# Moving the twiddle factors of a two-stage Fourier transform from the first-stage to the second-stage matrices

The kernel runs on one core of a Trainium2 chip. The metric is the time of one execution on the device, in microseconds (us).

## The reference

Eight sequences of 3008 tokens with 256 channels are filtered in frequency space, and the result goes through two matrix products.

```python
X = np.fft.rfft(x, axis=1)                      # x: (8, 3008, 256)
Y = X * (filt_r + 1j * filt_i)[None, :, :]
y = np.fft.irfft(Y, n=3008, axis=1)
h = y.reshape(24064, 256) @ w_in                # 256 -> 2048
out = np.maximum(0.01 * h, h) @ w_out           # 2048 -> 256
```

## The kernel before

3008 is 94 x 32. The first stage is a sum over 94 points on TensorE, the second a sum over 32 points. Between them each value is multiplied by a twiddle factor, a complex number of modulus 1 that depends on its place in both stages. Before, it stands in the first-stage matrices: one 94 x 128 matrix for each of the 32 columns of x, 786 KB in all. The second stage has one 128 x 128 matrix.

Batch 0 is transformed alone, ahead of everything else. Batches 1 to 7 are transformed in small groups between the matmuls of the two products (called MoE here).

```python
for i in range(FP):                                          # FP = 4 pieces on SyncE's queue
    nc.sync.dma_start(f1_sb[:, ts(i, step), :], f1_d.ap()[i])
nc.sync.dma_start(small_sb[:], small_d.ap())
first_parts = ((0, 10), (10, 10), (20, 8), (28, 4))          # columns of x: parts 0 to 3
for n0, nn in first_parts:
    x_load(0, n0, nn)                                        # GpSimd's queue, f32 to f16
for hf in range(2):                                          # filter halves 0 and 1
    filt_load(fa_sb, filt_r, hf * DH, DH)
    filt_load(fb_sb, filt_i, hf * DH, DH)
...
keep_warm(28)                                                # matmuls on zeros
for n0, nn in first_parts:
    # first stage of this part, copies out of PSUM by VectorE and ScalarE
    keep_warm(5 if n0 < N2 else 14)
t1_part(0, 0, True)(), t1_part(0, 1, True)()                 # transposes on VectorE
# load of the inverse matrices i1, second stage with filter products,
# inverse stages, then the MoE loop
```

The warm-up matmuls are there to keep TensorE's clock up while it waits for x.

Of the kernel before, what the change touches and what calls it, by code (L numbers as in the profile page):

```python
# [10 lines left out]
P = 128  # L11
FP16 = mybir.dt.float16
# [6 lines left out]
N1, N2 = 94, 32  # L19
NC = 24  # L20
Q = 32
R1 = 96
FP = 4


def _build_np_constants(N):
    n1, n2 = np.arange(N1), np.arange(N2)
    h = N2 // 2

    k2 = np.concatenate([np.arange(h), np.arange(N2 - 1, h - 1, -1)])  # L30

    sg = np.where(k2 < h, 1.0, -1.0)[None, :]
    th = 2 * np.pi * np.outer(n2, k2) / N2
    co, si = np.cos(th), np.sin(th)

    fwd1 = np.zeros((R1, N2, P))
    inv1 = np.zeros((P, N2, N1))
    fwd2, inv2 = np.zeros((P, P)), np.zeros((P, P))

    for s, (qr, qi) in enumerate(((0, 2), (1, 3))):  # L40
        k1 = NC * s + np.arange(NC)

        w = np.where((k1 == 0) | (k1 == N1 // 2), 1.0, 2.0)[:, None] / N1
        for j in n2:
            ang = 2 * np.pi * (np.outer(n1, k1) / N1 + j * k1[None, :] / N)
            fwd1[:N1, j, qr * Q : qr * Q + NC] = np.cos(ang)
            fwd1[:N1, j, qi * Q : qi * Q + NC] = -np.sin(ang)
            inv1[qr * Q : qr * Q + NC, j, :] = w * np.cos(ang).T
            inv1[qi * Q : qi * Q + NC, j, :] = -w * np.sin(ang).T

        cr, ci = (slice(64 * i + s, 64 * i + 64, 2) for i in range(2))
        r, i = (slice(Q * q, Q * q + Q) for q in (qr, qi))
        fwd2[r, cr], fwd2[i, cr] = co, si
        fwd2[r, ci], fwd2[i, ci] = -si * sg, co * sg
        inv2[cr, r], inv2[ci, r] = co.T, -(si * sg).T
        inv2[cr, i], inv2[ci, i] = si.T, (co * sg).T
    inv2 /= N2

    inv2x = np.concatenate([inv2[64:], -inv2[:64]], axis=0)
    small = np.stack([fwd2, inv2, inv2x], axis=1)  # L60
    fwd1 = fwd1.reshape(R1, FP, N2 // FP, P).transpose(1, 0, 2, 3)
    return (np.ascontiguousarray(fwd1).astype(np.float16), inv1.astype(np.float16), small.astype(np.float16))


@with_exitstack
def kernel(
# [9 lines left out]
    nc = tc.nc  # L76
    B, N, D = x.shape
# [7 lines left out]
    assert NCHUNK * CH == TOK  # L85
    SL = 8

    f1_np, i1_np, small_np = _build_np_constants(N)
    f1_d = nc.inline_tensor(f1_np, name="fwd1_const")
    i1_d = nc.inline_tensor(i1_np, name="inv1_const")  # L90
    small_d = nc.inline_tensor(small_np, name="small_const")

    cpool = ctx.enter_context(tc.tile_pool(name="const", bufs=1))
    f1_sb = cpool.tile([R1, N2, P], FP16, name="f1_sb")
    i1_sb = cpool.tile([P, N2, N1], FP16, name="i1_sb")
    small_sb = cpool.tile([P, 3, P], FP16, name="small_sb")
    fa_sb = cpool.tile([P, NC, D], FP16, name="fa_sb")
# [3 lines left out]
    x_sb = cpool.tile([P, N2, D], FP16, name="x_sb")  # L101
# [15 lines left out]
    def bank(kind, n, w):  # L117
        of = wide if kind == "ph" else single
        t = of[turn[kind] % len(of)]
        turn[kind] += 1  # L120
        return t[:, : n * w].rearrange("p (n w) -> p n w", n=n)

    ctx.enter_context(tc.manual_schedule())

    fwd2, inv2, inv2x = (small_sb[:, i, :] for i in range(3))

    DH = D // 2

# [8 lines left out]
    def filt_load(dst, src, d0, dn):  # L137

        for q, first, sgn in ((0, 0, 1), (Q, N1, -1)):
            nc.gpsimd.dma_start(  # L140
                dst[q : q + Q, :, ds(d0, dn)],
                bass.AP(tensor=src.tensor, offset=src.offset + first * D + d0,
                        ap=[[N1 * D, N2 // 2], [sgn * NC * D, 2], [sgn * D, NC], [1, dn]]))


    step = N2 // FP
    for i in range(FP):
        nc.sync.dma_start(f1_sb[:, ts(i, step), :], f1_d.ap()[i])
    nc.sync.dma_start(small_sb[:], small_d.ap())
    first_parts = ((0, 10), (10, 10), (20, 8), (28, 4))  # L150
    for n0, nn in first_parts:
# [1 line left out]
    for hf in range(2):  # L153
        filt_load(fa_sb, filt_r, hf * DH, DH)
        filt_load(fb_sb, filt_i, hf * DH, DH)
    nc.gpsimd.dma_start(w_in_sb[:], moe_w_in.rearrange("(dt p) c -> p dt c", p=P))
    idle = cpool.tile([P, CH], FP16, name="idle")
    nc.vector.memset(idle[:], 0.0)
# [8 lines left out]
    def s1_group(b, g, copy=nc.scalar.copy):  # L167
        def go():
            ps = bank("pf", 2, D)
            for j in range(2):  # L170
                n2 = 2 * g + j
                nc.tensor.matmul(ps[:, j, :], f1_sb[:N1, n2, :], x_sb[:N1, n2, :],  # L172
                                 start=True, stop=True)
            spread(big[(4 * b) % 3], 2 * g, ps, copy)
        return go


    def paired(t):
        return t[:].rearrange("p (e n t) -> p n e t", n=Q, t=2)

    def spread(dst, n0, ps, copy, e0=0):
        nn, de = ps.shape[1], ps.shape[2] // 2
        copy(paired(dst)[:, ds(n0, nn), ds(e0, de)], ps.rearrange("p n (e t) -> p n e t", t=2))  # L183
# [24 lines left out]
    def s2_group(b, g):  # L208
        def go():
            ps = bank("pf", 2, D)  # L210
            src = big[(4 * b + 1) % 3][:].rearrange("p (n d) -> p n d", n=Q)
            nc.tensor.matmul(ps, fwd2, src[:, ds(2 * g, 2), :], start=True, stop=True)  # L212
            fa, fb = fa_sb[:, ds(2 * g, 2), :], fb_sb[:, ds(2 * g, 2), :]
            p1 = scrp.tile([P, 2, D], FP32, tag="p1", name=f"p1_b{b}_g{g}")
            p2 = scrp.tile([P, 2, D], FP32, tag="p2", name=f"p2_b{b}_g{g}")
            nc.vector.tensor_tensor(p1[:], ps, fa, AL.mult)  # L216
            nc.vector.tensor_tensor(p2[0:64], ps[64:P], fb[64:P], AL.mult)  # L217
            nc.vector.tensor_tensor(p2[64:P], ps[0:64], fb[0:64], AL.mult)  # L218
            y1 = ypp.tile([P, 2, D], FP16, tag="y", name=f"y_b{b}_g{g}")
            nc.gpsimd.tensor_tensor(y1[:], p1[:], p2[:], AL.add)  # L220
            ys[(b, g)] = y1
        return go
# [25 lines left out]

    def first_s1(n0, n, kind, copy):
        ps = bank(kind, n, D)  # L250
        for j in range(n):
            nc.tensor.matmul(ps[:, j, :], f1_sb[:N1, n0 + j, :], x_sb[:N1, n0 + j, :],  # L252
                             start=True, stop=True)
        spread(big[0], n0, ps, copy)

# [5 lines left out]
    def first_s2(hf, c, n, kind, on_pool=False):  # L261
        ps = bank(kind, n, DH)
        src = paired(big[1])
        for j in range(0, n, 4):
            nc.tensor.matmul(ps[:, ds(j, 4), :].rearrange("p n (e t) -> p n e t", t=2), fwd2,  # L265
                             src[:, ds(c + j, 4), ts(hf, DH // 2)], start=True, stop=True)
        fs = [f[:, ds(c, n), ts(hf, DH)] for f in (fa_sb, fb_sb)]
        y = [prods[hf][:, i, ds(c, n), :] for i in range(2)]
        if on_pool:
            xs = [scrp.tile([P, 4, DH], FP32, tag=f"p{j // 4 + 1}", name=f"fx_h{hf}_c{c + j}")  # L270
                  for j in range(0, n, 4)]
            for j, xf in enumerate(xs):
                act(xf[:], ps[:, ts(j, 4), :])
            for i in range(2):
                for j, xf in enumerate(xs):
                    nc.gpsimd.tensor_tensor(y[i][:, ts(j, 4), :], xf[:], fs[i][:, ts(j, 4), :], AL.mult)
        else:
            for i in range(2):
                nc.vector.tensor_tensor(y[i], ps, fs[i], AL.mult)  # L279
# [28 lines left out]
    def upper(hf, t, copy):  # L308
        copy(t[64:P, :, ts(hf, DH)], t[0:64, :, ts(hf, DH)])


    def keep_warm(n):
        for _ in range(n):
            nc.tensor.matmul(po_ps.rearrange("p a d -> p (a d)"), idle[:, 0:P], idle[:],  # L314
                             start=True, stop=True)

    keep_warm(28)
    g = 0
    for n0, nn in first_parts:
        while nn:  # L320
            n = 2 if nn % 4 or n0 >= N2 - 4 else 4
            first_s1(n0, n, two[n // 4], (dve, act)[g % 2])
            n0, nn, g = n0 + n, nn - n, g + 1
        keep_warm(5 if n0 < N2 else 14)
    t1_part(0, 0, True)(), t1_part(0, 1, True)()

    nc.vector.memset(i1_sb[:, 0, 0:2], 0.0)
    nc.sync.dma_start(i1_sb[:], i1_d.ap())
    upper(0, fa_sb, act), upper(0, fb_sb, dve)
    first_s2(0, 8, 8, "ph", True)  # L330
    t1_part(0, 2, True)()
    first_s2(0, 0, 8, "ph")
    for n0 in (0, N2 // 2):
        x_load(1, n0, N2 // 2)
    t1_part(0, 3, True)()
    upper(1, fa_sb, act)
    first_s2(0, 16, 4, "pf"), first_s2(0, 20, 4, "pf")
    upper(1, fb_sb, dve)
    keep_warm(4)
# [89 lines left out]
    for slot in range(SL * (NCHUNK + 1)):  # L429
        ci, g = divmod(slot, SL)  # L430
# [36 lines left out]
```

## Time and profile before

| | before |
|---|---|
| time, median of the first 3 runs | 783.67 us (783.07 to 783.7) |
| span of the profiled execution | 780.9 us |
| TensorE busy | 771.9 us, 99% of the span |
| first MoE matmul starts | 41.50 us |
| from there to the end | 739.4 us |

### The profile page before, as it was taken

To read this page: it belongs to the slowest core of one execution; us is meant where nothing else is said; L and a number is where in the kernel's file an instruction comes from. 1 tells how busy PE (TensorE), PEld (TensorE's weight loads), DVE (VectorE), ACT (ScalarE), POOL (GpSimd) and SP (SyncE) were. 2 spreads that over 40 slices of the span, in tenths; PEclk is the share of its full clock that TensorE was granted. 3 is DMA by queue.
4 is the path that set the end of the run, shared out by engine and by line. 5 is a ranking of instruction groups with operands and counts; after the bars stand their busy time and mean duration, and the time that the engine had idled before them with its cause. 6 is when DMAs were issued, how large, how long until landed. Compare 5 with 4: busy or idle time off the path is not lost.

```text
span 780.9 us, 13401 instructions
## 1 busy us (share of the span) xinstructions
PE 771.9 (99%) x5710; PEld 523.9 (67%) x5710; DVE 369.5 (47%) x468; ACT 553.7 (71%) x784; POOL 146.4 (19%) x120
## 2 busy tenths in 40 slices
PE   9899999999999999999999999999999999999998
PEld 4366677666776677666777667766677666766666
DVE  4979751865238641576307744087432765200000
ACT  4777768676786767777587776967668776666664
POOL 4764300340004300042002410025000330000000
PEclk9999999999999999999999999999999999999999
DMA  9942003310141101510105010140101001110111
GB/s 189 217 79 74 28 28 68 82 38 32 41 95 42 42 28 42 108 41 29 41 28 122 28 42 28 41 107 28 42 28 42 28 31 38 41 38 31 41 41 55
DMA packets 36364, 43.38 MB, mean 56 GB/s; under 512 B 8146, under 2 KB 34386, under 8 KB 35538
## 3 DMA queue, kind: packets, MB, share of 16 engines
q0 software_dynamic: 9968, 16.22, 12.2%
q1 hardware_dynamic: 26336, 26.30, 9.6%
q8 instruction: 44, 0.72, 0.4%
q14 instruction: 16, 0.13, 0.1%
HBM read 34.10 MB, written 24.64 MB: 75 GB/s over the span
## 4 chain that ended last, share of the span: by engine, by line
PE 94%; ACT 1%; DVE 1%; issue 0%
PE ph L375 41%; PE po_ps L389 41%; PE pf L172 3%; PE pf L239 2%; PE pf L227 2%; PE pf L212 2%; PE pf L389 1%; ACT big L183 0%; DVE prod L279 0%; PE pf L286 0%; DVE big L294 0%; PE ph L303 0%; ACT yt L306 0%; ACT gt_c L380 0%; PE ph L265 0%
## 5 line engine op out<-in xcount | busy, mean ns | idle before, releaser
L380 ACT ACTIVATE gt_c<-ph 128x1024 f16<-128x1024 f32 x376 | 385.2, 1025 | 195.2 <-PE ph L375 193.8
L375 PE MATMUL ph<-yt,w_in_sb 128*128 128x512 f16 (+3 forms) x1600 | 386.4, 366 | 0.3
L389 PE MATMUL po_ps<-w_out_sb,gt_c 128*128 128x256 f16 x2944 | 381.5, 272 | 0.5 <-ACT ost_c_t L396 0.5
L389 PEld LDWEIGHTS <-gt_c 128*128 128x128 f16 x3008 | 290.8, 98 | 89.2 <-issue 1.8
L375 PEld LDWEIGHTS <-w_in_sb 128*128 128x128 f16 x1600 | 154.5, 98 | 95.7 <-issue 0.4
L220 POOL TENSOR_TENSOR y_b_g<-p_b_g,p_b_g 128x512 f16<-128x512 f32 x84 | 106.9, 1272 | 225.0 <-DVE p_b_g L218 225.0
L195 DVE STREAM_TRANSPOSE big<-big 128x1024 f32<-128x1024 f32 x32 | 55.9, 1846 | 126.1 <-ACT big L183 126.1
L183 ACT CAST big<-pf 128x512 f16<-128x512 f32 x186 | 106.5, 603 | 1.1 <-PE pf L252 1.1
L242 DVE CAST yt<-pf 128x376 f16<-128x376 f32 x112 | 56.4, 545 | 86.1 <-PE pf L239 86.1
L216 DVE TENSOR_TENSOR p_b_g<-pf,fa_sb 128x512 f32<-128x512 f32 x84 | 58.1, 692 | 37.7 <-PE pf L212 35.1
L396 ACT COPY ost_c_t<-po_ps 128x256 f32<-128x256 f32 x184 | 69.3, 376 | 6.5 <-PE po_ps L389 5.3
L203 DVE STREAM_TRANSPOSE big<-big 128x1024 f32<-128x1024 f32 x28 | 51.0, 1933 | 34.4 <-ACT big L183 34.4
L217 DVE TENSOR_TENSOR p_b_g<-pf,fb_sb 64x512 f32<-64x512 f32 x84 | 58.2, 692 | 1.1
L218 DVE TENSOR_TENSOR p_b_g<-pf,fb_sb 64x512 f32<-64x512 f32 x84 | 57.4, 683 | 1.1
L132 POOL DMA_DIRECT2D x_sb<-in_x_dram x13 | 7.1, 548 | 253.9 <-PE pf L172 253.1
L239 PEld LDWEIGHTS <-big 128*128 128x128 f16 x448 | 25.6, 98 | 13.2
L172 PE MATMUL pf<-x_sb,f_sb 94*128 94x256 f16 x224 | 33.9, 272 | 0.2 <-DVE yt L242 0.2
L212 PE MATMUL pf<-big,small_sb 128*128 128x512 f16 x84 | 31.8, 379 | 0.0
L227 PE MATMUL pf<-y_b_g,small_sb 128*128 128x512 f16 x84 | 31.8, 379 | 0.0
L172 PEld LDWEIGHTS <-f_sb 94*128 94x128 f16 x224 | 21.5, 97 | 12.4 <-issue 0.4
L239 PE MATMUL pf<-i_sb,big 128*128 128x94 f16 x448 | 28.7, 206 | 0.0
L314 PE MATMUL po_ps<-idle 128*128 128x512 f16 x66 | 17.5, 414 | 1.2 <-DVE one L161 1.2
(49 smaller groups left out, 157.9 us busy)
## 6 DMA issues: line engine op xcount, KB each, us to landing
out_dram<-ost_c_t SPq DMA_DIRECT2D x92, 256.0 KB, 2.1
x_sb<-in_x_dram POOLq DMA_DIRECT2D x5, 1536.0 KB, 10.9
x_sb<-in_x_dram POOLq DMA_DIRECT2D x2, 768.0 KB, 9.7
x_sb<-in_x_dram POOLq DMA_DIRECT2D x3, 480.0 KB, 8.8
w_in_sb<-in_moe_w_in_dram POOLq DMA_DIRECT2D x1, 1024.0 KB, 14.7
w_out_sb<-in_moe_w_out_dram POOLq DMA_DIRECT2D x1, 1024.0 KB, 9.7
x_sb<-in_x_dram POOLq DMA_DIRECT2D x1, 1024.0 KB, 8.2
f_sb<-fwd_const SPq DMA_DIRECT2D x4, 192.0 KB, 5.5
```

What stands on the lines that cost most here:

```text
L172: nc.tensor.matmul(ps[:, j, :], f1_sb[:N1, n2, :], x_sb[:N1, n2, :], start=True, stop=True)
L183: copy(paired(dst)[:, ds(n0, nn), ds(e0, de)], ps.rearrange("p n (e t) -> p n e t", t=2))
L216: nc.vector.tensor_tensor(p1[:], ps, fa, AL.mult)
L217: nc.vector.tensor_tensor(p2[0:64], ps[64:P], fb[64:P], AL.mult)
L218: nc.vector.tensor_tensor(p2[64:P], ps[0:64], fb[0:64], AL.mult)
L220: nc.gpsimd.tensor_tensor(y1[:], p1[:], p2[:], AL.add)
L239: nc.tensor.matmul(ps[:, j, :], src[:, dt, n2, :], i1_sb[:, n2, :], start=True, stop=True)
L242: copy(yv[:, :, ds(4 * h, 4)], ps.rearrange("p c a -> p a c"))
L375: nc.tensor.matmul(ph[:, j, ds(o, ln)], w_in_sb[:, dt, ts(ct, P)], yt[:, dt, ds(lo, ln)], start=(dt == 0), stop=(dt == NDT - 1),)
L380: nc.scalar.activation(gts[ci][:, ds(2 * g, 2), :], ph, AF.Lrelu)
L389: nc.tensor.matmul(po, gts[ci][:, ct, ts(tj, P)], w_out_sb[:, ct, :], start=(ct == 0), stop=(ct == NCT - 1))
L396: nc.scalar.copy(ost[:, tj % 2, :], po)
```

## The change

The intent: with the twiddle in the second stage, the first stage needs a single matrix, which fits into the 96 KB of small matrices. So x can load with nearly nothing beside it, and the new second-stage matrices (24 of 128 x 128, again 786 KB) come later, behind filter half 0. The warm-ups ahead of the first part go from 28 to 14, as x is expected earlier, and the inverse matrices are released later. The core of the diff (the numpy that builds the matrices, the renamings, and the same two edits in batch 0's own two stages are cut):

```diff
-    step = N2 // FP
-    for i in range(FP):
-        nc.sync.dma_start(f1_sb[:, ts(i, step), :], f1_d.ap()[i])
     nc.sync.dma_start(small_sb[:], small_d.ap())
...
         filt_load(fb_sb, filt_i, hf * DH, DH)
+        for i in (1, 0, 2) if hf == 0 else ():
+            nc.gpsimd.dma_start(f2_sb[:, ts(i, NC // FP), :], f2_d.ap()[i])
...   first stage, batches 1 to 7
-            for j in range(2):
-                n2 = 2 * g + j
-                nc.tensor.matmul(ps[:, j, :], f1_sb[:N1, n2, :], x_sb[:N1, n2, :], start=True, stop=True)
+            nc.tensor.matmul(ps, fwd1[:N1], x_sb[:N1, ds(2 * g, 2), :], start=True, stop=True)
...   second stage, batches 1 to 7
-            nc.tensor.matmul(ps, fwd2, src[:, ds(2 * g, 2), :], start=True, stop=True)
+            for j in range(2):
+                nc.tensor.matmul(ps[:, j, :], f2_sb[:, 2 * g + j, :], src[:, 2 * g + j, :],
+                                 start=True, stop=True)
...   head
-    keep_warm(28)
+    keep_warm(14)
...
     t1_part(0, 0, True)(), t1_part(0, 1, True)()
-    nc.vector.memset(i1_sb[:, 0, 0:2], 0.0)
-    nc.sync.dma_start(i1_sb[:], i1_d.ap())
     upper(0, fa_sb, act), upper(0, fb_sb, dve)
     first_s2(0, 8, 8, "ph", True)
     t1_part(0, 2, True)()
     first_s2(0, 0, 8, "ph")
+    nc.vector.memset(i1_sb[:, 0, 0:2], 0.0)
+    nc.sync.dma_start(i1_sb[:], i1_d.ap())
```

More of the change, by code (lines that the diff above doesn't have):

```diff
@@ L22 @@
 R1 = 96
-FP = 4
+FP = 3
 def _build_np_constants(N):
@@ L34, in _build_np_constants @@
     co, si = np.cos(th), np.sin(th)
-    fwd1 = np.zeros((R1, N2, P))
+    fwd1 = np.zeros((P, P))
+    fwd2 = np.zeros((P, NC, P))
     inv1 = np.zeros((P, N2, N1))
-    fwd2, inv2 = np.zeros((P, P)), np.zeros((P, P))
+    inv2 = np.zeros((P, P))
     for s, (qr, qi) in enumerate(((0, 2), (1, 3))):
         k1 = NC * s + np.arange(NC)
+        cr, ci = (slice(64 * i + s, 64 * i + 64, 2) for i in range(2))
+        r, i = (slice(Q * q, Q * q + Q) for q in (qr, qi))
+        ang = 2 * np.pi * np.outer(n1, k1) / N1
+        fwd1[:N1, qr * Q : qr * Q + NC] = np.cos(ang)
+        fwd1[:N1, qi * Q : qi * Q + NC] = -np.sin(ang)
+        for c in range(NC):
+            t = th + 2 * np.pi * n2[:, None] * k1[c] / N
+            fwd2[r, c, cr], fwd2[i, c, cr] = np.cos(t), np.sin(t)
+            fwd2[r, c, ci], fwd2[i, c, ci] = -np.sin(t) * sg, np.cos(t) * sg
         w = np.where((k1 == 0) | (k1 == N1 // 2), 1.0, 2.0)[:, None] / N1
         for j in n2:
-            ang = 2 * np.pi * (np.outer(n1, k1) / N1 + j * k1[None, :] / N)
-            fwd1[:N1, j, qr * Q : qr * Q + NC] = np.cos(ang)
-            fwd1[:N1, j, qi * Q : qi * Q + NC] = -np.sin(ang)
-            inv1[qr * Q : qr * Q + NC, j, :] = w * np.cos(ang).T
-            inv1[qi * Q : qi * Q + NC, j, :] = -w * np.sin(ang).T
-        cr, ci = (slice(64 * i + s, 64 * i + 64, 2) for i in range(2))
-        r, i = (slice(Q * q, Q * q + Q) for q in (qr, qi))
-        fwd2[r, cr], fwd2[i, cr] = co, si
-        fwd2[r, ci], fwd2[i, ci] = -si * sg, co * sg
+            t = ang.T + 2 * np.pi * j * k1[:, None] / N
+            inv1[qr * Q : qr * Q + NC, j, :] = w * np.cos(t)
+            inv1[qi * Q : qi * Q + NC, j, :] = -w * np.sin(t)
         inv2[cr, r], inv2[ci, r] = co.T, -(si * sg).T
@@ L59, in _build_np_constants @@
     inv2x = np.concatenate([inv2[64:], -inv2[:64]], axis=0)
-    small = np.stack([fwd2, inv2, inv2x], axis=1)
-    fwd1 = fwd1.reshape(R1, FP, N2 // FP, P).transpose(1, 0, 2, 3)
-    return (np.ascontiguousarray(fwd1).astype(np.float16), inv1.astype(np.float16), small.astype(np.float16))
+    small = np.stack([fwd1, inv2, inv2x], axis=1)
+    fwd2 = fwd2.reshape(P, FP, NC // FP, P).transpose(1, 0, 2, 3)
+    return (np.ascontiguousarray(fwd2).astype(np.float16), inv1.astype(np.float16), small.astype(np.float16))
 @with_exitstack
@@ L86 @@
     SL = 8
-    f1_np, i1_np, small_np = _build_np_constants(N)
-    f1_d = nc.inline_tensor(f1_np, name="fwd1_const")
+    f2_np, i1_np, small_np = _build_np_constants(N)
+    f2_d = nc.inline_tensor(f2_np, name="fwd2_const")
     i1_d = nc.inline_tensor(i1_np, name="inv1_const")
@@ L93 @@
     cpool = ctx.enter_context(tc.tile_pool(name="const", bufs=1))
-    f1_sb = cpool.tile([R1, N2, P], FP16, name="f1_sb")
+    f2_sb = cpool.tile([P, NC, P], FP16, name="f2_sb")
     i1_sb = cpool.tile([P, N2, N1], FP16, name="i1_sb")
@@ L123 @@
     ctx.enter_context(tc.manual_schedule())
-    fwd2, inv2, inv2x = (small_sb[:, i, :] for i in range(3))
+    fwd1, inv2, inv2x = (small_sb[:, i, :] for i in range(3))
     DH = D // 2
@@ L169, in go @@
             ps = bank("pf", 2, D)
-            for j in range(2):
-                n2 = 2 * g + j
-                nc.tensor.matmul(ps[:, j, :], f1_sb[:N1, n2, :], x_sb[:N1, n2, :],
-                                 start=True, stop=True)
+            nc.tensor.matmul(ps, fwd1[:N1], x_sb[:N1, ds(2 * g, 2), :], start=True, stop=True)
             spread(big[(4 * b) % 3], 2 * g, ps, copy)
@@ L250, in first_s1 @@
         ps = bank(kind, n, D)
-        for j in range(n):
-            nc.tensor.matmul(ps[:, j, :], f1_sb[:N1, n0 + j, :], x_sb[:N1, n0 + j, :],
+        for j in range(0, n, 2):
+            nc.tensor.matmul(ps[:, ds(j, 2), :], fwd1[:N1], x_sb[:N1, ds(n0 + j, 2), :],
                              start=True, stop=True)
@@ L263, in first_s2 @@
         src = paired(big[1])
-        for j in range(0, n, 4):
-            nc.tensor.matmul(ps[:, ds(j, 4), :].rearrange("p n (e t) -> p n e t", t=2), fwd2,
-                             src[:, ds(c + j, 4), ts(hf, DH // 2)], start=True, stop=True)
+        for j in range(n):
+            nc.tensor.matmul(ps[:, j, :].rearrange("p (e t) -> p e t", t=2), f2_sb[:, c + j, :],
+                             src[:, c + j, ts(hf, DH // 2)], start=True, stop=True)
         fs = [f[:, ds(c, n), ts(hf, DH)] for f in (fa_sb, fb_sb)]
```

## The prediction

> **What bounds the kernel now.** I read the page first (busy shares and the chain of waits), then the timeline of the main loop, then the timeline, the waits and the landing of each transfer in the first 45 us.
>
> ```profile
> PE 771.9 (99%) x5710; PEld 523.9 (67%) x5710; DVE 369.5 (47%) x468; ACT 553.7 (71%) x784; POOL 146.4 (19%) x120
> ...
> PE 94%; ACT 1%; DVE 1%; issue 0%
> ...
> 53.95 1.03 PE L375 MATMUL ph<-yt,w_in_sb 128*128 128x512 f16 x4
> ...
> 54.81 1.04 PE L389 MATMUL po_ps<-w_out_sb,gt_c 128*128 128x256 f16 x8
> ...
> 55.69 1.03 PE L375 MATMUL ph<-yt,w_in_sb 128*128 128x512 f16 x4
> ```
>
> TensorE is busy 99% and is 94% of the chain. That alone does not say it is at its peak; the last three lines do. One slot of the main loop (4 matmuls of 512 columns and 8 of 256) repeats after 55.69 - 53.95 = 1.74 us. It streams 4096 columns, 1.707 us at 2.4 columns per ns, and the other 0.03 us over 12 matmuls is some 2.4 ns each. The whole main loop is 770,048 columns in each of the two MoE products, 57,344 in the first transform stage of seven batches, 43,008 in each of the two second stages and 42,112 in the last inverse stage: 1,725,568 columns, at 1.735 us per 4096 some 731 us. Measured it is 777.3 - 41.5 = 736 us. So the main loop has perhaps 5 us of slack in all and nothing but columns can move it. What is left is the **head**, the 41.5 us before the first MoE matmul, in which batch 0 is transformed with nothing to overlap it.
>
> ```profile
> 1.20 8.11 PE L314 MATMUL po_ps<-idle 128*128 128x512 f16 x28 [1.20 <-DVE one L161]
> ...
> 8.93 1.19 PEld L252 LDWEIGHTS <-f_sb 94*128 94x128 f16 x10
> ...
> 10.13 0.86 PEld L314 LDWEIGHTS <-idle 128*128 128x128 f16 x5
> ...
> 11.10 1.19 PEld L252 LDWEIGHTS <-f_sb 94*128 94x128 f16 x10
> ...
> 13.28 0.10 PEld L252 LDWEIGHTS <-f_sb 94*128 94x128 f16 x1
> ...
> 16.81 2.37 DVE L195 STREAM_TRANSPOSE big<-big 128x1024 f32<-128x1024 f32 x2 [0.22 <-ACT big L183]
> ```
>
> Here the reader sees that the head up to 16.8 us is a TensorE queue: 28 warm-up matmuls on zeros, then the ten columns of x part 0, five warm-ups, part 1 at 11.10, five warm-ups, part 2 at 13.28, and no gap: 10 x 0.1075 + 5 x 0.2155 = 2.15 us, and 8.93 + 2.15 = 11.08, 11.10 + 2.15 = 13.25. The transfers land only a little before they are used. From 16.81 us VectorE takes over:
>
> ```profile
> DVE yt L306 <- ACT yt L306: 0.7, 1, 0.7
> DVE prod L279 <- PE pf L265: 0.7, 1, 0.7
> DVE yt L306 <- PE ph L303: 0.3, 1, 0.3
> DVE big L195 <- ACT big L183: 0.2, 1, 0.2
> ```
>
> These are all waits of VectorE from 16.8 to 41.5 us, 1.9 us in total. So transposes, filter products and copies run one behind the other from 16.81 to 38.3 us; if that chain starts earlier, and each filter and matrix has landed when its turn comes, the MoE starts earlier by the same amount.
>
> **When transfers land** (issue plus time to landing, by the tile view for each issue): x parts 0 to 3 at 7.9, 10.7, 12.8 and 13.8 us; filter half 0 at 14.9, 16.1 (real), 17.1, 18.2 (imaginary); half 1 at 19.2, 21.2, 22.2, 23.3; the four pieces of the old first-stage matrices at 3.3, 3.8, 10.1 and 12.6, the small matrices at 13.9, w_in at 29.9, the inverse matrices at 28.0.
>
> ```profile
> q0 software_dynamic: 148, 0.68, 81.9%
> q1 hardware_dynamic: 144, 0.26, 18.9%
> ```
>
> That is the DMA view from 4.0 to 8.2 us: the x queue moved 0.68 MB in 82% of the engines' time, the matrices 0.26 MB in 19%. The engines are full, so each byte of the old matrices delays x.
>
> **What the Trainium skill says.** "TensorE: Matmul & The Clock Gate", section "Back-to-back issue gap", gives N / 2.4 + 2.5 ns for a warm matmul; the 2.4 ns above agree. The same page, section "What's actually happening", says that an idle TensorE falls to half clock and that some 3.4 us of work bring it back. The trace agrees: the 28 warm-ups start 0.43 us apart and go to 0.21 us from 5.0 us, and after an idle stretch at 22.8 to 24.9 us the granted clock is 0.50 from 26 to 28 us. "DMA: Bandwidth & Descriptors", section "Queues, rings and completion order", says that each DMA engine takes turns between the queues at packet granularity, so a second queue takes time from the first; the two lines above show both sharing.
>
> **The change part by part.**
>
> 1. *Main loop.* First stage: 224 matmuls of 256 columns become 112 of 512. Second stage: 84 of 512 become 168 of 256. The columns are the same, the matmuls 28 fewer: 28 x 2.4 ns = 0.07 us. Weight loads stay hidden (in the second MoE product a 256-column matmul with a new matrix runs at 0.87 / 8 = 0.109 us, 256 / 2.4 + 2.4 ns). Worth nothing.
>
> 2. *Warm-ups 28 to 14.* The 14 taken away are warm ones, at (8.80 - 5.01) / 18 = 0.21 us: TensorE reaches part 0 at 8.93 - 14 x 0.2135 = 5.94 us, 2.99 us earlier. This is the most the head can gain.
>
> 3. *x without the matrices beside it.* Up to 14 us the matrices hold the engines for about 0.79 us (18.9% of 4.2 us), some 0.65 us before that while x was already queued (0.41 MB had moved by 4 us, in 32.3% of 4 us = 1.3 us, half of it before x's packets began), and for the 0.21 MB after 8.2 us some 0.64 us at the same rate. So x parts come earlier by 1.4, 1.7, 1.95 and 2.1 us: 6.5, 9.0, 10.9 and 11.7 us. The small matrix, now first on its queue, lands near 3.3 as the old first piece did. TensorE then starts part 0 at 6.5 (0.6 us idle), part 1 at max(9.0, 6.5 + 2.15) = 9.0, part 2 at max(10.9, 9.0 + 2.15) = 11.15. Before it was 13.28, so VectorE's chain starts **2.1 us** earlier by this account, and up to 3.0 if x comes faster than reckoned. I take 2.5: chain start at 14.3.
>
> 4. *The new second-stage matrices.* The 786 KB are not gone, they stand behind filter half 0 on the x queue. Filter half 0 moves forward to some 12.8, 14.0, 15.0 and 16.1 us. A 262 KB piece at the 300 GB/s that the windows at 23 to 27 us show takes 0.9 us: pieces 1, 0, 2 land at about 17.0, 17.9 and 18.7. Needed: piece 1 when the second transpose ends, 14.3 + 2.4 = 16.7; piece 0 before VectorE's first product at 21.39 - 2.5 = 18.9, with about 0.9 us of TensorE work ahead of it (17.9 + 0.9 = 18.8); piece 2 at 22.3. So it fits with almost no margin, and I charge 0.3 us. Issuing is no limit: the ninth transfer on that queue waited for the first to land, the tenth for the second and so on, and so would the new ones, each before its turn.
>
> 5. *Second-stage matmuls of batch 0.* 24 of 128 columns in place of 6 of 512 for each half. The old ones took 0.43 us each, twice their columns' time[...]; the same columns at the same stride cost the same, 0.86 us per eight. In the last inverse stage a 94-column matmul with its own 128-column load took 0.51 us less 0.17 of drain, over 8, some 0.043 us, so the loads hide.
>
> 6. *Filter half 1 and what follows.* As many bytes stand ahead of it as before, so it lands at about the same clock time, near 23 us, helped a little as the inverse matrices no longer start at 19.2 us but after VectorE's first products. Its real part is copied by ScalarE (2.75 us, has until 28.24 - 2.5 = 25.7) and its imaginary part by VectorE at 27.26 - 2.5 = 24.8: both have 1.5 us or more to spare. The inverse matrices, issued near 21.2 with 8.8 us to landing, arrive at 30, needed at 33.6.
>
> Sum: -2.5 + 0.3 - 0.07, about -2.3 us, and 783.67 - 2.3 = **781.4 us**.
>
> **Rivals.** *A, a wait on the new matrices takes the place of the one removed.* For it: the margin of step 4 is near zero, and one more microsecond there goes straight into the VectorE chain. Against it: pieces are ordered as they are used. It would leave 0 to 1.3 us of gain: 782.4 to 783.7. *B, x comes as fast as TensorE is ready,* as its transfers no longer share any engine: the full 3.0 us, and if the half-clock stretch at 26 to 28 us also goes, the 0.7 us that VectorE waited for a matmul after it: 780.0 to 780.7. *C, the half clock spreads:* TensorE idles longer ahead of the second stage, and the stage's matmuls run at half rate; against it speaks that the 14 warm-ups ahead of the first transpose stay. It would cost about 1 us: 782.4 or more. *D, the main loop changes* by more columns or exposed loads: the count in step 1 speaks against it.
>
> **Range and chances.** The head can hardly give more than 3.7 us nor lose more than 1; executions differ by 0.6. So 779.7 to 783.3. Two per cent are 15.7 us, more than a third of the whole head: faster 0.01, slower 0.01.
>
> **What would show it.** Right: first MoE matmul near 39.2 in place of 41.5 us; x part 0 landing near 6.5 and TensorE idle a little before it; first VectorE transpose at 14 to 14.7; VectorE's waits on second-stage matmuls under 1 us; main loop within 0.5 us of 736. Wrong: a VectorE or TensorE wait of over 1 us ending near 17 to 19 us on the new matrices (rival A), filter half 1 landing after 25 us, or a main loop that changes by more than 1 us.

## The result and the profile after

| | before | after |
|---|---|---|
| time, median (4 runs each) | 783.68 us (783.07 to 783.93) | 780.14 us (779.54 to 780.91) |
| span of the profiled execution | 780.9 us | 778.8 us |
| first MoE matmul starts | 41.50 us | 39.36 us |
| from there to the end | 739.4 us | 739.4 us |

The ratio is 0.9957 (95% interval 0.9939 to 0.9974). A ratio here is the mean time of one kernel's runs over that of the other's of the same rounds, so not quite the ratio of the medians. The time falls within the predicted range. The gain of 0.4% is clear of the noise, but far below the 2% at which a run would be called faster.

The page of the changed kernel, busy shares and chain of waits:

```profile
PE 768.5 (99%) x5688; PEld 521.5 (67%) x5688; DVE 369.6 (47%) x468; ACT 553.5 (71%) x784; POOL 148.7 (19%) x123
...
PE 96%; DVE 2%; ACT 1%; DMA 1%; issue 0%; DVEq 0%; POOLq 0%
```

TensorE is the bound as before. A transfer is now in the chain for 1%; before there was none. The view by stretches of time, first the kernel before, then the changed one (after the stretch come its length, then busy time and count of instructions of TensorE, weight loads, VectorE, ScalarE and GpSimd, then granted clock, DMA share and GB/s):

```profile
45.00:775.00 730.00, 729.23 (x5411) 501.80 (x5410) 338.06 (x430) 526.46 (x745) 116.32 (x92) 1.00 0.17 47
```
```profile
45.00:775.00 730.00, 729.23 (x5397) 500.05 (x5394) 336.70 (x427) 524.47 (x743) 113.72 (x92) 1.00 0.17 48
```

The main loop is as full as before, 729.23 us of 730 in both. So the time came from the head. TensorE's and VectorE's timeline of the changed head (start, length, then what released the engine):

```profile
1.20 4.48 PE L316 MATMUL po_ps<-idle 128*128 128x512 f16 x14 [1.20 <-DVE one L164]
7.07 0.38 PE L254 MATMUL pf<-x_sb,small_sb 94*128 94x512 f16 x1 [1.39 <-DMA x_sb<-in_x_dram]
...
9.30 0.38 PE L254 MATMUL pf<-x_sb,small_sb 94*128 94x512 f16 x1
...
11.50 1.02 PE L254 MATMUL ph<-x_sb,small_sb 94*128 94x512 f16 x4
...
14.77 2.37 DVE L195 STREAM_TRANSPOSE big<-big 128x1024 f32<-128x1024 f32 x2 [0.21 <-ACT big L183]
...
17.19 1.92 PE L267 MATMUL ph<-big,f_sb 128*128 128x128 f16 x16
...
39.36 1.31 PE L377 MATMUL ph<-yt,w_in_sb 128*128 128x512 f16 x4
```

TensorE now waits 1.39 us for part 0 of x, where before its warm-ups ran until the data had long landed. The three part starts are 7.07, 9.30 and 11.50 us in place of 9.14, 11.31 and 13.53, and VectorE's chain (the row of transposes, products and copies that the prediction follows) starts at 14.77 in place of 16.81. The DMA view of the changed kernel from 4.0 to 8.2 us, to be laid beside the two lines for this stretch in the prediction:

```profile
q0 software_dynamic: 192, 0.85, 101.8%
```

The x queue now has the engines to itself and moves 0.85 MB where it moved 0.68 before. From there VectorE's chain is as long as it was: to the first MoE matmul it is 39.36 - 14.77 = 24.59 us, and 41.50 - 16.81 = 24.69 before. VectorE waits as little as before, in all 1.7 us:

```profile
DVE yt L308 <- ACT yt L308: 0.7, 1, 0.7
DVE prod L281 <- PE pf L267: 0.6, 1, 0.6
DVE yt L308 <- PE ph L305: 0.2, 1, 0.2
DVE big L195 <- ACT big L183: 0.2, 1, 0.2
```

So the two profiles show a gain of 2.1 us, but the medians show 3.5. That gap is the question of the first experiments.

### The profile page after: what moved, and what is told of

The parts are those of the page before. It is cut to its first block, busy times and chain, and to the rows that moved or that the text cites. A ratio compares the mean times of both kernels' runs of the same rounds, so it can differ in the third digit from the quotient of the medians.

```text
span 778.8 us, 13329 instructions
## 1 busy us (share of the span) xinstructions
PE 768.5 (99%) x5688; PEld 521.5 (67%) x5688; DVE 369.6 (47%) x468; ACT 553.5 (71%) x784; POOL 148.7 (19%) x123
## 4 chain that ended last, share of the span: by engine, by line
PE 96%; DVE 2%; ACT 1%; DMA 1%; issue 0%; DVEq 0%; POOLq 0%
PE ph L377 41%; PE po_ps L391 41%; PE pf L173 3%; PE pf L241 2%; PE pf L213 2%; PE pf L229 2%; PE pf L391 1%; DMA x_sb<-in_x_dram 1%; DVE big L195 1%; DVE prod L281 1%; PE pf L288 0%; ACT big L183 0%; PE po_ps L316 0%; PE ph L267 0%; PE ph L254 0%
## 5 line engine op out<-in xcount | busy, mean ns | idle before, releaser
L173 PE MATMUL pf<-x_sb,small_sb 94*128 94x512 f16 x112 | 33.6, 380 | 0.2 <-DVE yt L244 0.2
L213 PE MATMUL pf<-big,f_sb 128*128 128x256 f16 x168 | 32.1, 273 | 0.0
L213 PEld LDWEIGHTS <-f_sb 128*128 128x128 f16 x168 | 16.4, 98 | 19.7
L173 PEld LDWEIGHTS <-small_sb 94*128 94x128 f16 x112 | 10.7, 98 | 10.5
```

Source lines behind the costliest of these rows:

```text
L173: nc.tensor.matmul(ps, fwd1[:N1], x_sb[:N1, ds(2 * g, 2), :], start=True, stop=True)
L213: nc.tensor.matmul(ps[:, j, :], f2_sb[:, 2 * g + j, :], src[:, 2 * g + j, :], start=True, stop=True)
```

## The experiments

Every run was correct and had five timed executions; the medians of the kernel before in the same session on one chip stand beside them. In all traces the span less the start of the first MoE matmul is 739.3 to 739.6 us, so the head is all that these edits move. "Part 0 lands" is its issue plus its time to landing; "chain" is VectorE's first transpose.

| run | part 0 lands | TensorE starts it | chain | first MoE | median us | before |
|---|---|---|---|---|---|---|
| before, first trace | 7.9 | 9.14 | 16.81 | 41.50 | 783.68 | |
| before_again | 9.2 | 10.14 | 17.81 | 42.31 | 783.59 | 783.30 |
| before_warm14 | 9.3 | 9.33 | 18.66 | 43.35 | 784.51 | 783.27 |
| before_fill | 9.4 | 9.46 | 17.84 | 41.74 | 783.06 | 783.30 |
| before_small_first | 7.7 | 9.32 | 16.98 | 41.68 | 783.12 | 783.15 |
| after, first trace | 7.0 | 7.07 | 14.77 | 39.36 | 780.14 | 783.68 |
| after_again | 6.6 | 6.76 | 14.39 | 39.37 | 780.58 | 783.27 |
| after_warm28 | 7.2 | 10.05 | 17.68 | 42.28 | 783.31 | 783.27 |
| after_f2_sync | 7.6 | 7.62 | 15.93 | 40.53 | 781.58 | 783.27 |
| after_old_bytes | 8.1 | 8.19 | 16.79 | 41.64 | 782.20 | 783.28 |
| after_i1_early | 6.7 | 6.76 | 14.49 | 38.71 | 780.49 | 783.30 |
| after_fill | 6.9 | 6.91 | 14.62 | 38.57 | 779.99 | 783.30 |
| after_fill_short | 6.9 | 6.96 | 14.11 | 38.53 | 779.80 | 783.28 |
| after_tuned | 6.7 | 6.94 | 13.96 | 38.01 | 779.39 | 783.28 |

### The changed kernel again (after_again)

No edit.

> The changed kernel once more, five rounds, so that all variants of this call stand beside it on the same chip. The two profiles give 2.1 us of gain, all of it in the head (first MoE matmul at 39.36 in place of 41.50 us), but the medians 3.5 us. Theory 1 (head plus clock): the head is worth 2.1 us in every run and the remaining 1.4 us is which executions have the half-clock stretch of TensorE in the head (two of the four runs of the change had a granted clock of 1.000 and a span of 777.8, the other two 0.997 and 778.8); then runs of clock 1.000 are 1.0 us shorter than the rest, and the gain between runs of equal clock is 2.1 us, some 781.6 against 783.7 at the lower clock. Rival: a real further gain of 1.4 us that the profiled execution does not show; then the runs of lower clock gain 3 us or more too.

Measured: 780.58 us (779.85 to 781.12), ratio 0.9963 to before. Theory 1 in this first form fell. Runs of equal clock differ by far more than 2.1 us: at a granted clock of 1.000 (the mean share of TensorE's full clock in an execution) the spans of before in this call are 781.1 and 781.3 and that of the change is 777.9, some 3.3 us apart; at 0.997 and 0.998 they are 781.0 to 782.2 against 778.6 to 779.2. So the rival was right: most runs gain nearly 3 us. As the main loop is the same in every trace, the profiled execution of before had to be one with a short head.

### The kernel before again (before_again)

No edit.

> The kernel before, unchanged, for a second trace of it and five more times. In every trace so far the span less the start of the first MoE matmul is 739.3 to 739.5 us, so each run's span tells the length of its head: 41.6 to 42.8 us for the runs of before so far (mean near 42.0), 38.4 to 39.8 for those of the change (mean near 39.1), and the profiled run of before, 41.5, was the shortest of all. Theory 1 (amended): before varies as its 28 warm-ups end at 8.9 to 10.1 us, according to when the clock goes up (5.0 us in its profile, about 7.0 in the change with 28 warm-ups), and x part 0 lands at 7.9 to 9.3; this trace then has its head at 41.6 to 42.8, clock up or x part 0 later than in the first trace, and its first transpose later than 16.81 by the same amount, within 0.5. Rival: the longer runs lose their time in the half-clock stretch or in the main loop; then the first transpose is at 16.8 and the difference comes after it.

Measured: 783.59 us (782.58 to 784.53). Its trace, to be laid beside the first one in the prediction:

```profile
1.20 9.11 PE L314 MATMUL po_ps<-idle 128*128 128x512 f16 x28 [1.20 <-DVE one L161]
...
10.14 0.38 PE L252 MATMUL pf<-x_sb,f_sb 94*128 94x256 f16 x2
...
17.81 2.37 DVE L195 STREAM_TRANSPOSE big<-big 128x1024 f32<-128x1024 f32 x2 [0.22 <-ACT big L183]
```

The same 28 warm-ups took 9.11 us in place of 8.11, as their spacing went from 0.43 to 0.21 us only at 7.1 us in place of 5.0, and part 0 landed at 9.2 us in place of 7.9. The first transpose is 1.0 us later and the first MoE matmul 0.8 us later. This is theory 1 as amended: the head of before varies at its very start, and the trace that I predicted from was an early one. Over all 41 runs of before the spans are 780.6 to 782.5, mean 781.4; the profiled one was 780.9.

### Half of the change each way (after_warm28, before_warm14)

```diff
after_warm28:                          before_warm14:
-    keep_warm(14)                     -    keep_warm(28)
+    keep_warm(28)                     +    keep_warm(14)
```

> The changed kernel with 28 warm-up matmuls before the first x part again in place of 14. Theory 1: the first transform stage then waits for TensorE's own queue: part 0 starts at 8.93 us, part 1 at 11.08, part 2 at 13.23 as before, VectorE's chain at 16.8 in place of 14.77, first MoE matmul near 41.4, so 2.0 us slower than the change. Rival (transfers alone made the gain): less than 0.5 us slower than the change.

Measured: 783.31 us, ratio 0.9995 (0.9983 to 1.0008) to before. The whole gain is gone, 2.7 us and not the 2.0 stated: part 0 had landed at 7.2 us, but TensorE came to it only at 10.05, as in this trace the clock went up late and the 28 warm-ups took 9.02 us.

```profile
1.20 9.02 PE L316 MATMUL po_ps<-idle 128*128 128x512 f16 x28 [1.20 <-DVE one L164]
...
10.05 0.38 PE L254 MATMUL pf<-x_sb,small_sb 94*128 94x512 f16 x1
```

> The kernel before with 14 warm-up matmuls in place of 28 and nothing else changed. Theory 1: x parts still share the engines with the first-stage matrices and land at 7.9, 10.7, 12.8 and 13.8 us, so TensorE idles for the first part but part 1 starts at 10.8 to 11.0 and part 2 at 13.0 to 13.2: VectorE's chain starts 0 to 0.3 us earlier, time 783.4 to 783.9. Rival (the 28 warm-ups alone held the head back): 2 to 3 us faster, 780.7 to 781.7.

Measured: 784.51 us, ratio 1.0012 (1.0000 to 1.0025): no gain, rather a loss, outside the range I gave. The trace shows why it is worse:

```profile
9.33 0.49 PE L252 MATMUL pf<-x_sb,f_sb 94*128 94x256 f16 x2 [2.56 <-DMA x_sb<-in_x_dram]
9.62 1.92 PE L252 MATMUL ph<-x_sb,f_sb 94*128 94x256 f16 x8
11.32 2.02 PE L314 MATMUL po_ps<-idle 128*128 128x512 f16 x5
13.18 0.38 PE L252 MATMUL pf<-x_sb,f_sb 94*128 94x256 f16 x2
```

TensorE idled 2.56 us for part 0, and then eight matmuls took 1.92 us in place of the 1.03 of the other traces: the granted clock had fallen (0.50 from 10 to 12 us), and part 1 started at 13.18. The fall is not the only thing that kept this run from a gain: part 2 landed only at 14.3 us, later than TensorE came to it in the first trace of before (13.53). All five runs have a granted clock of 0.995 or 0.996, lower than any other kernel's here.

So before had **two limits close together**: the warm-ups, which ended between 8.7 and 10.3 us, and x, which landed between 7.7 and 9.4 us. Lifting either one alone gives nothing.

### The new matrices beside x (after_f2_sync)

```diff
     nc.sync.dma_start(small_sb[:], small_d.ap())
+    for i in (1, 0, 2):
+        nc.sync.dma_start(f2_sb[:, ts(i, NC // FP), :], f2_d.ap()[i])
...
-        for i in (1, 0, 2) if hf == 0 else ():
-            nc.gpsimd.dma_start(f2_sb[:, ts(i, NC // FP), :], f2_d.ap()[i])
```

> The changed kernel with its 786 KB of second-stage matrices moved back to where the first-stage matrices stood: on SyncE's queue from the start, beside x, right after the small matrices. Same arithmetic, same bytes, 14 warm-ups. Theory 1: these bytes take engine time from x again, x parts land at 7.9, 10.7, 12.8 us as before, VectorE's chain starts at 16.4 to 16.8 and 1.7 to 2.0 us of the 2.1 us are lost. Rival (what counts is that the first stage needs no matrix beyond the small one, not where the bytes stand): x lands within 0.5 us of the change's 7.0, 9.1, 11.2 us and the time stays within 0.5 us of the change's.

Measured: 781.58 us, 1.0 us slower than the change and 1.7 faster than before. The direction is theory 1's: parts 0, 1 and 2 of x started at 7.62, 10.46 and 12.66 us, each right after its transfer, where the change has 7.07, 9.30 and 11.50:

```profile
7.62 0.38 PE L254 MATMUL pf<-x_sb,small_sb 94*128 94x512 f16 x1 [1.23 <-DMA x_sb<-in_x_dram]
...
10.46 0.38 PE L254 MATMUL pf<-x_sb,small_sb 94*128 94x512 f16 x1 [0.52 <-DMA x_sb<-in_x_dram]
```

(For part 2 only the weight load waited, 0.36 us, and the warm-ups before it ran until then.) The size was not: I had charged the whole gain to these bytes, and more than half of it stays. With 14 warm-ups TensorE takes each part as it lands, and in this trace part 2 landed 0.9 us before the 28 warm-ups of before would have let TensorE come to it (13.53 in its first trace). It landed earlier, too, than in most traces of before; the next two runs look into that.

### Loads of the old shape (after_old_bytes)

```diff
+    old_sb = cpool.tile([R1, 32, P], FP16, name="old_sb")
     nc.sync.dma_start(small_sb[:], small_d.ap())
+    for i in range(4):
+        nc.sync.dma_start(old_sb[:, ts(i, 8), :], old_d.ap()[i])
```

(old_d holds the same numbers as the new matrices in the old shape; nothing reads the buffer.)

> The changed kernel with four more loads on SyncE's queue right after the small matrices, of the shape of the old first-stage matrices (4 of 192 KB on 96 partitions), into a buffer that nothing reads; the new matrices stay where the change put them. It is to find why the new matrices on SyncE's queue (3 of 256 KB on 128 partitions, run before) cost 1.0 us where I had expected 1.7 to 2.0: x part 0 landed at 7.6 us there, against 7.9, 9.1, 9.4 and 9.2 us in four traces with the old matrices. If the shape or number of the old loads is what slows x: x part 0 lands at 8.9 to 9.4, VectorE's chain starts at 17.3 to 17.9 and the time is within 0.6 us of before. If it is their order (the small matrices last) or chance: x part 0 at 7.4 to 8.0, chain start near 16, time 781.3 to 782.0.

Measured: 782.20 us, part 0 at 8.1, chain at 16.79. Neither reading fits: the landing is between both. These bytes beside x leave 1.1 us of gain over before, where the change had 2.7 in its call, though part of that comes later: the first second-stage matmul waited for its matrix until 19.51 us.

### The order of the old loads (before_small_first)

```diff
+    nc.sync.dma_start(small_sb[:], small_d.ap())
     for i in range(FP):
         nc.sync.dma_start(f1_sb[:, ts(i, step), :], f1_d.ap()[i])
-    nc.sync.dma_start(small_sb[:], small_d.ap())
```

> The kernel before with the 96 KB of small matrices loaded ahead of the four pieces of the first-stage matrices in place of after them, as the kernels with early landings (x part 0 at 7.6 us with the new matrices on SyncE's queue, 8.2 with loads of the old shape behind the small ones) have it. If the order is what slows x in before: part 0 at 8.2 us or earlier and 0.5 us or more faster than before. If not: part 0 at 9.0 to 9.5 us, with VectorE's chain at 17.4 to 17.9, and the time within 0.4 us of before; the cause of the unlike landings then stays open.

Measured: 783.12 us, ratio 0.9998 (0.9984 to 1.0011). Part 0 landed early, at 7.7 us, as in the first trace of before, but the time did not move: TensorE's warm-ups held it until 9.32. This shows the second limit without any change of x. Whether the order made x early, or chance as in the first trace, one trace cannot tell; why x lands at 7.9 in one execution of before and at 9.2 in another **stays open**. It is not that the matrices took more in the slow one: from 4.0 to 8.2 us before_again moved fewer packets of both queues, 128 of x and 123 of the matrices, where the first trace moved 148 and 144.

### The later inverse matrices (after_i1_early)

```diff
+    nc.vector.memset(i1_sb[:, 0, 0:2], 0.0)
+    nc.sync.dma_start(i1_sb[:], i1_d.ap())
     upper(0, fa_sb, act), upper(0, fb_sb, dve)
...
-    nc.vector.memset(i1_sb[:, 0, 0:2], 0.0)
-    nc.sync.dma_start(i1_sb[:], i1_d.ap())
```

> The changed kernel with the load of the inverse matrices put back to its old place, released after the second transpose (near 17 us) in place of after VectorE's first products (21.6 us). Theory 1: it shares engine time with filter half 1, which lands up to 0.8 us later (21.5 and 23.8 us), but ScalarE's copy has until 25.2 and VectorE's until 25.2, so the time stays within 0.3 us of the change's. Rival (this move was part of the gain): 0.5 us or more slower, with VectorE waiting near 25 us for filter half 1.

Measured: 780.49 us, ratio 0.9962 to before, against 0.9957 and 0.9963 for the change. The imaginary part of filter half 1 landed at 24.3 us in place of 23.0, later than I had said, but VectorE came to it only at 25.19 and did not wait. This part of the change is worth nothing by itself.

### The gap with the falling clock (before_fill, after_fill)

```diff
-    keep_warm(4)
+    keep_warm(12)
```

> The kernel before with 12 in place of 4 warm-up matmuls in the gap of TensorE at 21.8 to 24.9 us, to keep its clock up. Theory 1: granted clock 1.000 in all runs, the half-clock stretch at 26 to 28 us is gone, 0.3 to 1.0 us faster than before (782.4 to 783.1); its spread from the first warm-ups stays. Rival (the half clock costs nothing, as VectorE is the bound there): clock 1.000 and the time within 0.2 us.

Measured: 783.06 us, ratio 0.9997 (0.9985 to 1.0010): clock 1.000 in all five runs, no clear gain in time. In its trace the 28 warm-ups were over at 8.7 us, the earliest of all, and yet nothing came of it, as now x was the limit at parts 0 and 1:

```profile
9.46 0.38 PE L252 MATMUL pf<-x_sb,f_sb 94*128 94x256 f16 x2 [0.73 <-DMA x_sb<-in_x_dram]
...
12.36 0.38 PE L252 MATMUL pf<-x_sb,f_sb 94*128 94x256 f16 x2 [0.57 <-DMA x_sb<-in_x_dram]
```

After that the fill did help in this trace: from VectorE's first transpose to the first MoE matmul it is 41.74 - 17.84 = 23.90 us, against 24.69 and 24.50 in the two traces of before. The late x hid it.

> The changed kernel with the same 12 in place of 4 warm-ups in the same gap (19.8 to 22.9 us). Theory 1: clock 1.000 in all runs, spans 777.6 to 778.0 as the two undisturbed runs of the change had, 779.5 to 779.9 us, 0.6 to 1.0 faster than the median of the change and with less spread. Then the change is worth 2.5 to 3.3 us beside the kernel before with the same fill. Rival: within 0.2 us of the change.

Measured: 779.99 us (779.80 to 780.02), a little above the range given; all spans 778.0 or 778.1, clocks 0.999 or 1.000. That is 0.55 us below the median of the nine runs of the change (780.54) and 0.50 below after_i1_early, the change without this fill, and the spread falls from 1.6 us (the nine runs) to 0.2. The stretch of 24 to 28 us, first the changed kernel, then this one (the third number from the end is the granted clock):

```profile
24.00:26.00 2.00, 2.00 (x13) 1.32 (x12) 1.97 (x3) 1.21 (x3) 0.51 (x1) 0.58 1.05 260
26.00:28.00 2.00, 2.00 (x6) 0.71 (x5) 1.97 (x3) 1.87 (x4) 1.35 (x2) 0.57 1.12 318
```
```profile
24.00:26.00 2.00, 2.00 (x15) 1.37 (x14) 1.97 (x3) 1.55 (x3) 0.37 (x1) 1.00 1.05 260
26.00:28.00 2.00, 1.63 (x10) 0.80 (x9) 1.97 (x3) 2.00 (x6) 1.80 (x2) 1.00 1.02 304
```

With the gap filled the clock stays up. From VectorE's first transpose to the first MoE matmul it takes 38.57 - 14.62 = 23.95 us here and 39.36 - 14.77 = 24.59 in the change. With both gaps filled the change is worth 3.1 us (means of 783.06 against 779.93).

### Fewer warm-ups between the parts, and the matrix that then comes late (after_fill_short, after_tuned)

```diff
both, besides the filled gap:
-        keep_warm(5 if n0 < N2 else 14)
+        keep_warm({10: 5, 20: 4, 28: 1}.get(n0, 14))
after_tuned also:
         filt_load(fa_sb, filt_r, hf * DH, DH)
+        if hf == 0:
+            nc.gpsimd.dma_start(f2_sb[:, ts(1, NC // FP), :], f2_d.ap()[1])
         filt_load(fb_sb, filt_i, hf * DH, DH)
-        for i in (1, 0, 2) if hf == 0 else ():
+        for i in (0, 2) if hf == 0 else ():
...
-    upper(0, fa_sb, act), upper(0, fb_sb, dve)
-    first_s2(0, 8, 8, "ph", True)
-    t1_part(0, 2, True)()
+    upper(0, fa_sb, act)
+    t1_part(0, 2, True)()
+    upper(0, fb_sb, dve)
+    first_s2(0, 8, 8, "ph", True)
```

> The changed kernel with the gap filled (12 in place of 4 warm-ups) and fewer warm-ups between the x parts: 4 in place of 5 ahead of part 2 and 1 in place of 5 ahead of part 3, as part 3 lands at 12.0 to 12.3 us but TensorE reaches it at 13.1 to 13.6. Theory 1: VectorE's chain starts 0.5 us earlier, at 14.1, but piece 1 of the second-stage matrices still lands at 17.0, which was just in time and now is not: VectorE's first product moves 0.2 us and not 0.5; 779.6 to 779.9 us. Rival (matrices have room): 779.3 to 779.5.

Measured: 779.80 us (779.59 to 780.24). The chain starts at 14.11, 0.5 us earlier, but the second stage could not follow:

```profile
17.09 1.92 PE L267 MATMUL ph<-big,f_sb 128*128 128x128 f16 x16 [0.94 <-DMA f_sb<-fwd_const]
...
19.11 1.22 DVE L281 TENSOR_TENSOR prod<-ph,fa_sb 128x1024 f16<-128x1024 f32 x1 [0.19 <-issue]
```

TensorE waited 0.94 us for piece 1 of the new matrices, and VectorE's first product is at 19.11 in place of 19.17 in after_fill. Here is my rival A, a wait on the new matrices: in the change it was just out of sight.

> The same, with piece 1 of the second-stage matrices loaded ahead of the imaginary half of filter half 0, and VectorE's copy of that half after its third transpose in place of before it. Theory 1: piece 1 lands near 15.2 us, the first second-stage matmul starts at 16.5, and the full 0.5 us is gained: 779.3 to 779.5 us, fastest of all. Rival: the later filter or the third transpose holds VectorE and it is no faster than the version without this reordering.

Measured: 779.39 us (779.24 to 779.46), ratio 0.9948 (0.9936 to 0.9961), the fastest of all and ahead of both kernels. VectorE's first product starts at 18.57:

```profile
13.96 3.50 DVE L197 STREAM_TRANSPOSE big<-big 128x1024 f32<-128x1024 f32 x3 [0.21 <-ACT big L185]
17.49 0.95 DVE L313 COPY fb_sb<-fb_sb 64x3072 f16<-64x3072 f16 x1
18.57 1.22 DVE L283 TENSOR_TENSOR prod<-ph,fa_sb 128x1024 f16<-128x1024 f32 x1
```

Of the two halves of this edit (the matrix earlier, the copy later) no run tells which did more.

## Why the prediction was right or wrong

The range held the result (780.14 in 779.7 to 783.3), near its lower end. The mechanism was right; the gain was larger than the 2.3 us stated: 3.5 us by the medians of the first runs, 2.7 in after_again, 2.9 between the means of all 41 and all 9 runs (783.33 and 780.39). That the first two profiles show almost exactly the 2.1 us worked out is in part luck, as steps 2 and 3 show. Of the signs that the prediction named, the first MoE matmul (39.36 us), the idle TensorE before part 0 and the small wait on second-stage matmuls (0.6 us) came as stated; part 0 of x (7.0 us) and the first transpose (14.77) were a little late.

- **Step 1, main loop: right.** 739.4 us from the first MoE matmul to the end in both kernels. The formula taken from the skill is given there for an isolated matmul; here the stream fits it too.
- **Step 2, warm-ups: right that they had to go, wrong in that 2.99 us was fixed.** The 28 warm-ups took 8.11, 9.11 and 7.53 us (first trace of before, before_again, before_fill), by when the clock went up. (The 0.2135 us for one warm-up is in no line; 0.2155, which the prediction has elsewhere, gives 3.02 us.) after_warm28 shows that without this cut nothing is gained.
- **Step 3, x without the matrices beside it: the term that was mis-sized.** I worked 2.1 us out of one trace of before and took 2.5. The chain starts at 16.81, 17.81, 17.84 and 16.98 us in four traces with 28 warm-ups and the old matrices (mean 17.36), and at 14.77, 14.39, 14.62 and 14.49 in four with the change's start (mean 14.57): 2.8 us earlier. What failed is the base: the landings I took as fixed (7.9, 10.7 us) were the early end of a spread; part 0 lands at 7.7 to 9.4 us with the old matrices and at 6.6 to 7.2 in the kernels with the change's loads. Between the two first traces the landings moved by less than stated: 0.9, 1.45, 1.7 and 1.7 us for parts 0 to 3, where I had 1.4, 1.7, 1.95 and 2.1. Two errors worked against each other.
- **Step 4, the new matrices: right in the landings, and the charge of 0.3 us was not needed.** Pieces 1, 0 and 2 landed at 17.1, 17.9 and 18.8 us against 17.0, 17.9 and 18.7 stated. The first second-stage matmul started at 17.19, right as the second transpose ended at 17.14. after_fill_short shows the near-zero margin to be real.
- **Step 5: right.** Eight matmuls of 128 columns took 0.93 us in the chain, against 0.86 stated: some twice the time of their columns, as before the change. Why they take twice that, no run tests.
- **Step 6: right in what mattered.** Filter half 1 landed until 23.0 us, the inverse matrices at 31.8 (I had said 30), and VectorE waited for neither; ScalarE waited 1.5 us for the real half of the filter, within its slack.
- **Rivals.** B, the full 3 us, came nearest, and its reasons hold in some executions only: in the first trace TensorE did wait for x (1.39 us), but in after_again its 14 warm-ups ran on until it took part 0 at 6.76 us; and the half-clock stretch went in three of the nine runs of the change (clock 1.000), as in seven of 41 of before. C did not come about: the stretch is there in both kernels. When it is absent the head of the change is some 0.6 us shorter by the traces of after_fill and the change, and some 1.0 by the spans (777.8 to 777.9 us at clock 1.000, 778.6 to 779.2 in the other six runs).

What stays open: why x lands at different times in different executions of the same kernel, and why the old bytes in the old place cost more than the new bytes on the same queue (part 0 at 7.6 us there, 8.1 with loads of the old shape, up to 9.4 in before). So the bytes beside x are shown to cost 1.0 us (after_f2_sync) to 1.6 (after_old_bytes, where a late matrix is part of it) of the 2.7; what share of the rest is theirs, no run separates.

## What to carry to other kernels

Where a load and a fixed count of filler instructions end at about the same time, neither alone shows what the other costs: shorten both, and test each half. When a kernel is filled to 99% by one engine, look at what nothing overlaps, here 5% of the time. And a head of transfers should be read from several executions before a gain of 1 us is worked out from it: here one trace of before was 0.5 us shorter than the mean and that of the change 0.3 longer (778.8 against 778.5), which hid over a quarter of the gain.

## What the Trainium skill lacked or had wrong

- "TensorE: Matmul & The Clock Gate", section "What you observe", puts the clock's rise at about 4 us into the work, give or take 0.5 us from run to run. Here the spacing of the warm-ups, which start at 1.2 us, changed at 3.7 us (before_fill), 5.0 us (first trace of before) and 7.1 us (before_again), so 2.5 to 5.9 us into the work; that it varies by run the page says further on. It matters for warm-ups of a fixed count: 28 of them took 7.53 to 9.11 us.
- The same page, section "Why this matters for your kernels", warns of idle gaps over about 3 us. Here gaps of 2.56 us (before_warm14) and 2.07 us (first trace of before) were followed by half the clock, while one of 2.27 us (after_i1_early) was not.
- "DMA: Bandwidth & Descriptors", section "Queues, rings and completion order", says that each engine takes turns between queues packet by packet. This agrees: from 4 to 8.2 us in before, GpSimd's queue sent 148 packets and SyncE's 144 (152 and 149 in after_f2_sync, 145 and 145 in after_old_bytes). What the section does not draw out is that time then goes by the size of the packets: 82% for x with 0.68 MB, 19% for the matrices with 0.26 MB. The small matrices landed 11.3 us after their issue there and 1.9 us after it in the change, where they came first.
- On no page that I read: the ninth transfer that this kernel issues on GpSimd's queue is issued only when the first has landed (at 8.2 us in before, 7.3 in the change), the tenth after the second, and so on. In the trace's records the ninth reports its landing on the semaphore of the first, with eight in turn, so this may come from how the program was built and not from the chip.
